# Turning the next tile's tokens: TensorE's transposes against VectorE's 32x32 transposes and a way through DRAM

## The chip, the cores and the metric

One core of a Trainium2 chip runs the whole program. The time is device microseconds of one execution, as the median of several runs; the profiler gives one execution in detail. The engines are TensorE (PE, with its weight loads PEld), VectorE (DVE), ScalarE (ACT), GpSimd (POOL) and SyncE (SP), which here issues every DMA.

## The reference

For 8 batches of 576 tokens with 8 heads of 64: attention of 32 pack tokens over the keys, and of the queries over the packed values; the heads are joined to 512 features. Then a mixing step (real part of a Fourier transform over tokens and features, added to x), a normalization of each token, and a feed-forward net with its input added again:

```
X = np.fft.fft(np.fft.fft(x, axis=1), axis=2)
u = x + np.real(X)
un = (u - mean(u)) / sqrt(var(u) + 1e-6)
out = u + np.maximum(un @ w_ch1, 0.0) @ w_ch2        # w_ch1 512 x 2048, w_ch2 2048 x 512
```

All of it is fp32.

## The kernel before

The 4608 tokens are handled as 36 blocks of 128, kept in `ubuf` (128 tokens x 512 features). Of each batch come four blocks, (E,0), (O,0), (E,1), (O,1), and of each pair of batches one more, R, with the tokens left over. Nine tiles, 0 to 8, take four blocks each, in that order, so a tile can straddle batches: tile 2 holds R of the first pair and three blocks of batch 2, tile 6 holds two blocks of batch 5, an R, and one of batch 6.

`ffn` is the feed-forward net of one tile, 16 turns (`j`) over the 2048 hidden features. Each fp32 factor is used as two fp32r parts, a high one and a low one (`split`: ScalarE casts the high part, then VectorE or GpSimd subtracts to get the low one), and each product takes three matmuls. In turn j, `up(j)` is 12 matmuls of 128x128 by 128x512 into the one PSUM buffer `ph`; ScalarE makes `hh` (relu, L653) and VectorE `hl` (L654) from it. Then `down(j-1)` is 12 matmuls into the accumulators `acc` (L664). `wsplits` splits the weights, two parts per turn, `wr_h` on ScalarE (L99) and `wr_l` on GpSimd (L100), with room for three weights at a time; each `next(splits)` is one of them.

`up` needs the tokens transposed, features on the partitions: `uh` and `ul`, 128 x 4 x 512, one buffer each. The class `Turned` makes them for the next tile at the end of this one: `less(i)` subtracts the mean (VectorE, L601, tile `un`), `moves(i)` are four TensorE transposes of 128x128 (L608, into PSUM `untp`), handed out one by one between the matmuls of `up(15)`, `down(14)` and `down(15)`, and `parts(i)` splits the result into `uh` (ScalarE) and `ul` (VectorE). The scale of the normalization is applied at the end of the tile (L700), where the output is stored too.

`front(b)` is everything ahead of that for batch b: attention, spectra, and the blocks `u`. It is a generator, run a piece at a time by `step(i)`, i from 0 to 31, two steps per turn, while the tile before is in `ffn`. For tiles from 1 on, front(t+1) begins at step 1; (E,0) and (O,0) come at step 26, (E,1) and (O,1) at step 28, and R in steps 0 and 2 of the next tile (`rest`). The order on TensorE, VectorE, ScalarE and GpSimd is that of the program text for all tiles but the first; each of the engines works off its list in order. `after(n, what)` puts work off by n steps: the squares of `statistics` come one step after the block, the power two steps after.

From step 12 to step 21 VectorE has the softmax's end and the folding of the weights (`m`, `a`, `f`, `r`, `h` in `ORDER`: L393 to L397, L425, L427, L437 to L468, L481 to L485). DMA loads of keys, values and queries (`kp`, `vt`, `qt`) are on SP's queue.

Of the kernel before, what the change touches and what calls it, by code (L numbers as in the profile page):

```python
# [9 lines left out]
F32 = mybir.dt.float32  # L10
# [3 lines left out]
ALU = mybir.AluOpType  # L14
AX = mybir.AxisListType

P = 128
# [4 lines left out]
DM = 512  # L22
# [24 lines left out]
STG0 = [-2, -2, -4, -4, -6, -6]  # L47
STG1 = [9, None, None]
LEAD = 2
NJ = 16  # L50
MANUAL = {getattr(mybir.EngineType, n) for n in ("PE", "DVE", "Activation", "Pool")}
NE = 289
# [25 lines left out]
def tile_kernel(ctx, tc, kpT, qT, v, w1, w2, tabC, tabS, tabR, tabB, tabT, sel, ident_d, out):  # L78
    nc = tc.nc
# [4 lines left out]
    work = ctx.enter_context(tc.tile_pool(name="work", bufs=2))  # L84
    small = ctx.enter_context(tc.tile_pool(name="small", bufs=2))
    ps = ctx.enter_context(tc.tile_pool(name="ps", bufs=3, space=bass.MemoryType.PSUM))
    psf = ctx.enter_context(tc.tile_pool(name="psf", bufs=1, space=bass.MemoryType.PSUM))

    spare = ["acc0", "acc1", "acc2", "acc3"]
    nbank = [0]  # L90
# [7 lines left out]
    def split(hi, lo, src, lo_eng=None):  # L98
        nc.scalar.copy(hi, src)  # L99
        (lo_eng or nc.vector).tensor_tensor(lo, src, hi.bitcast(F32), ALU.subtract)  # L100
# [7 lines left out]
    for h in range(4):  # L108
        nc.gpsimd.memset(bmask[h * NPK:(h + 1) * NPK, h:h + 1], 0.5)
    w1f = cpool.tile([P, NJ, DM], F32, name="w1f")  # L110
    w2f = cpool.tile([P, NJ, DM], F32, name="w2f")

    nc.scalar.activation(small.tile([P, 1], F32, tag="ri", name="warm"), mhalf, AF.Exp)
    ubuf = cpool.tile([P, NU, DM], F32, name="ubuf")
    stages = (STG0 + STG1 * 40)[:2 * NJ]

# [35 lines left out]
    def spot(n, part, shape):  # L152

        t = (w1f, w2f)[n].rearrange("p j n -> p (j n)")[:, (part % NJ) * DM:]
        size = shape[1] * shape[2]
# [13 lines left out]
    def load_weights(j):  # L169

        for n, dst in enumerate((w1f, w2f)):
            if (j, n) not in fetched:
                fetch(j, n)
            st = fetched.pop((j, n))
            low, high = st[:, :, 0], st[:, :, 1]
            c = dst[:, j, :].bitcast(I32)


            nc.scalar.activation(c.bitcast(F32), high.bitcast(F32), AF.Prelu, scale=REBIAS, alpha=-2.0 ** 32)  # L179
            nc.vector.tensor_scalar(c, c, 3, None, ALU.logical_shift_left)  # L180
            nc.vector.scalar_tensor_tensor(c, low, 29, c, ALU.logical_shift_right, ALU.bitwise_or)  # L181
# [2 lines left out]


    u_of, stat_of, place_of, free = {}, {}, {}, list(range(NU))

    def new_u(key):
        place_of[key] = free.pop(0)
        u_of[key] = ubuf[:, place_of[key], :]  # L190

        stat_of[key] = small.tile([P, 4], F32, tag="stat", name="stat", bufs=12)
# [3 lines left out]
    steps = [None]  # L196

    def after(n, what):

        if steps[0] is None:  # L200
            what()
        else:
            due.append((steps[0] + n, what))
# [7 lines left out]
    def statistics(key):  # L211
        st, u = stat_of[key], u_of[key]
        nc.vector.tensor_scalar(st[:, 1:2], st[:, 0:1], 1.0 / DM, None, ALU.mult)  # L213

        def squares():
            junk = work.tile([P, DM], F32, tag="tmp", name="junk", bufs=3)
            nc.scalar.activation(junk, u, AF.Square, bias=st[:, 1:2], scale=-1.0, accum_out=st[:, 2:3])  # L217

        def deviation():
            nc.vector.tensor_scalar(st[:, 2:3], st[:, 2:3], 1.0 / DM, 1e-6, ALU.mult, ALU.add)  # L220
            nc.gpsimd.tensor_tensor(st[:, 2:3], st[:, 2:3], mhalf, ALU.pow)

        after(1, squares)
        after(2, deviation)
# [365 lines left out]
    class Turned:  # L590
# [2 lines left out]


        def __init__(self, keys):
            self.keys, self.un, self.tp, self.hl = keys, {}, {}, None

        def less(self, i):
            key = self.keys[i]
# [12 lines left out]
        def parts(self, i):  # L612
            if self.hl is None:
                self.hl = [work.tile([P, 4, 512], F32R, tag=n, name=n, bufs=1) for n in ("uh", "ul")]
            w = slice(i * P, (i + 1) * P)
            split(self.hl[0][:, :, w], self.hl[1][:, :, w], self.tp[i].rearrange("p (c t) -> p c t", c=4))

    def wsplits():

        for _ in tiles:  # L620
            for n, j in [(0, 0)] + [x for j in range(1, NJ) for x in ((0, j), (1, j - 1))] + [(1, NJ - 1)]:
                hi = work.tile([P, DM], F32R, tag="wr", name="wr_h", bufs=6)
                lo = work.tile([P, DM], F32R, tag="wr", name="wr_l", bufs=6)
                split(hi, lo, (w1f, w2f)[n][:, j, :], nc.gpsimd)
                ready.append((hi, lo))
                yield

    def ffn(first, turned, step, nxt, alone):
        keys = turned.keys
        n = len(keys)  # L630
        T = n * P
        uh, ul = turned.hl
        acc = [psf.tile([P, DM], F32, tag=f"acc{i}", name=f"acc{i}") for i in range(n)]
        now["acc"] = acc

        def up(j, moves=(), between=lambda: None):
            moves = list(moves)
            wh, wl = ready.pop(0)

            pool, tag = (ps, "ps") if alone and j % 2 else (psf, "ph")  # L640
            ph = pool.tile([P, 512], F32, tag=tag, name="ph")

            step = T // 2 if first == 0 and j < SPL else T
            for t in (slice(i, i + step) for i in range(0, T, step)):
                for k in range(12):
                    c, (l, r) = k // 3, ((wh, uh), (wh, ul), (wl, uh))[k % 3]
                    nc.tensor.matmul(ph[:, t], l[:, c * P:(c + 1) * P], r[:, c, t], start=(k == 0), stop=(k == 11))  # L647
                    if moves:
                        moves.pop(0)()
            between()  # L650
            hh = work.tile([P, 512], F32R, tag="hh", name="hh")
            hl = work.tile([P, 512], F32R, tag="hl", name="hl")
            nc.scalar.activation(hh[:, :T], ph[:, :T], AF.Relu)  # L653
            nc.vector.scalar_tensor_tensor(hl[:, :T], ph[:, :T], 0.0, hh[:, :T].bitcast(F32), ALU.max, ALU.subtract)  # L654
            return hh, hl

        def down(j, hh, hl, moves=()):

            moves = list(moves)
            vh, vl = ready.pop(0)  # L660
            for i in range(n):
                w = slice(i * P, (i + 1) * P)
                for k, (l, r) in enumerate(((hh, vh), (hh, vl), (hl, vh))):
                    nc.tensor.matmul(acc[i], l[:, w], r, start=(j == 0 and k == 0), stop=(j == NJ - 1 and k == 2))  # L664
                    if moves:
                        moves.pop(0)()

        def less(*ks):
            for k in ks:
                nxt.less(k)  # L670

        prev = None
        for j in range(NJ):
            last = nxt is not None and j == NJ - 1
            if last:
                cur = up(j, nxt.moves(0) + nxt.moves(1), lambda: less(2, 3))
                nxt.parts(0)
                nxt.parts(1)  # L680
            else:
                cur = up(j)
            next(splits, None)
            if nxt is not None and j == NJ - 2:
                less(0, 1)
            step(2 * j)
            if prev is not None:
                down(j - 1, *prev, [lambda: None] * 8 + nxt.moves(2) if last else ())
                if last:
                    nxt.parts(2)  # L690
                next(splits, None)
            step(2 * j + 1)
            prev = cur
        down(NJ - 1, *prev, nxt.moves(3) if nxt else ())
        if nxt:
            nxt.parts(3)
        next(splits, None)
        for i, key in enumerate(keys):
            u = u_of[key]
            nc.vector.scalar_tensor_tensor(u, acc[i], stat_of[key][:, 2:3], u, ALU.mult, ALU.add)  # L700
            nc.sync.dma_start(out[(first + i) * P:(first + i + 1) * P, :], u)
            free.append(place_of[key])

    keys = []
# [10 lines left out]
    cur = Turned(tiles[0][1])  # L715
# [8 lines left out]
    rest = iter(())  # L724
    for j in range(ORDER[0].count("D"), LEAD):
        load_weights(j)
    ready, splits = [], wsplits()
    next(splits)
    next(splits)
    for t, (first, tk) in enumerate(tiles):  # L730
# [4 lines left out]
        def step(i):  # L735

            next_step()
            if t > 0 and i in (0, 2):
                next(rest, None)
            elif not ended and next(gen, None) == "rest":  # L740
                ended.append(gen)
            if t == 0 and i % 2 == 0 and i // 2 + LEAD < NJ:
                load_weights(i // 2 + LEAD)
            assert i < 2 * NJ - 1 or t + 1 >= B or ended

        nxt = Turned(tiles[t + 1][1]) if t + 1 < len(tiles) else None
# [3 lines left out]
        cur, rest = nxt, gen  # L750
# [101 lines left out]
```

## Time and profile before

| what | value |
|---|---|
| time, median of 3 runs | 1028.04 us (1027.53 to 1029.04) |
| profiled execution, first to last instruction | 1025.3 us |
| left between that span and the median of the runs | 2.7 us |
| TensorE busy | 978.5 us (95%) |
| VectorE, ScalarE, GpSimd busy | 608.8, 425.0, 463.1 us |
| L608, transposes of the tokens on TensorE | 144, 37.2 us of busy time |
| mean granted TensorE clock | 0.983 |

For the profiled execution the page gives the span alone, and the sums of the prediction are made against it. A row of the page or of a view that groups instructions names the line, the engine, the operation, what it writes and reads, the count, then the busy time and the mean of one in ns, then the idle time ahead of them and what ended it. A row of a timeline has the start in us, the duration in us, engine, line, operation, tiles, and in brackets how long the engine had been idle before and which instruction released it. Durations of matmuls overlap, since they are pipelined; the distance between starts is the time that one takes.

### The profile page before, as it was taken

The numbers are of one execution on the slowest core, as the hardware profiler recorded it, in microseconds if no ns is written. First come the engines' busy times: TensorE is split into PE (matmuls) and PEld (weight loads), VectorE is DVE, ScalarE is ACT, GpSimd is POOL, SyncE is SP. The second block draws the span as 40 slices with busy tenths as digits, with TensorE's granted clock in tenths as the row PEclk, the third lists the DMA queues.
The fourth block names the chain that finished last, engine by engine and source line by source line (L and its number), as shares of the span: only waits on it lengthen the run. The fifth ranks groups of instructions, "written<-read, shape, count | busy, mean of one in ns | idle before, by whom it ended". The sixth has DMA issues, their size and how long they took to land.

```text
span 1025.3 us, 14876 instructions
## 1 busy us (share of the span) xinstructions
PE 978.5 (95%) x5692; PEld 795.6 (78%) x5692; DVE 608.8 (59%) x1264; ACT 425.0 (41%) x883; POOL 463.1 (45%) x419
## 2 busy tenths in 40 slices
PE   6489889999999999999999999999999999999998
PEld 2367668878877888788887887788778888887886
DVE  3897994559465856677556846594658562114112
ACT  2556454444443434444444435444435343333322
POOL 1535635364335534454345533643355344444443
PEclk9699899999999999999999999999999999999999
DMA  8328440220023000310041002200210000001001
GB/s 329 109 64 280 157 123 1 93 96 1 1 78 111 1 1 34 108 48 1 1 140 49 1 1 93 96 0 1 82 58 0 1 26 17 0 1 43 1 1 42
DMA packets 17742, 58.64 MB, mean 57 GB/s; under 512 B 2081, under 2 KB 2465, under 8 KB 17670
## 3 DMA queue, kind: packets, MB, share of 16 engines
q1 hardware_dynamic: 17670, 57.68, 16.4%
q8 instruction: 45, 0.74, 0.3%
q14 instruction: 27, 0.22, 0.1%
HBM read 48.24 MB, written 9.44 MB: 56 GB/s over the span
## 4 chain that ended last, share of the span: by engine, by line
PE 76%; DVE 11%; ACT 5%; DMA 3%; issue 2%; POOL 2%; ACTq 0%; SPq 0%; DVEq 0%; POOLq 0%
PE ph L647 35%; PE acc L664 30%; DVE ubuf L567 2%; DMA wst<-w 2%; DVE turned L419 1%; ACT hh L653 1%; PE po L326 1%; PE s L269 1%; ACT junk L217 1%; DVE turned L415 1%; POOL wr_l L100 1%; PE e1tp L303 1%; DVE hl L654 1%; ACT wr_h L99 1%; DVE w2f L181 1%
## 5 line engine op out<-in xcount | busy, mean ns | idle before, releaser
L100 POOL TENSOR_TENSOR wr_l<-w1f,wr_h 128x512 fp32r<-128x512 f32 x144 | 190.8, 1325 | 398.9 <-ACT wr_h L99 395.1
L654 DVE SCALAR_TENSOR_TENSOR hl<-ph,hh 128x512 fp32r<-128x512 f32 x144 | 98.8, 686 | 305.3 <-ACT hh L653 305.0
L647 PE MATMUL ph<-uh,wr_h 128*128 128x512 f32 (+1 forms) x580 | 231.5, 399 | 11.8 <-DVE hl L654 9.6
L100 POOL TENSOR_TENSOR wr_l<-w2f,wr_h 128x512 fp32r<-128x512 f32 x144 | 192.4, 1336 | 91.9 <-ACT wr_h L99 91.9
L664 PE MATMUL acc<-wr_l,hh 128*128 128x512 f32 x576 | 227.0, 394 | 3.0 <-POOL wr_l L100 3.0
L647 PE MATMUL ph<-uh,wr_l 128*128 128x512 f32 (+1 forms) x580 | 229.3, 395 | 0.4 <-POOL wr_l L100 0.4
L647 PE MATMUL ph<-ul,wr_h 128*128 128x512 f32 (+1 forms) x580 | 229.3, 395 | 0.2 <-DVE ul L100 0.2
L664 PE MATMUL acc<-wr_h,hh 128*128 128x512 f32 x576 | 227.8, 396 | 0.0
L664 PE MATMUL acc<-wr_h,hl 128*128 128x512 f32 x576 | 226.2, 393 | 0.0
L653 ACT ACTIVATE hh<-ph 128x512 fp32r<-128x512 f32 x144 | 85.8, 596 | 285.6 <-PE ph L647 285.4
L647 PEld LDWEIGHTS ph<-uh,wr_h 128*128 128x128 f32 x580 | 109.9, 190 | 44.9 <-DVE hl L654 9.8
L647 PEld LDWEIGHTS ph<-uh,wr_l 128*128 128x128 f32 x580 | 110.0, 190 | 24.7 <-POOL wr_l L100 0.8
L664 PEld LDWEIGHTS acc<-wr_l,hh 128*128 128x128 f32 x576 | 108.2, 188 | 26.8 <-POOL wr_l L100 5.4
L647 PEld LDWEIGHTS ph<-ul,wr_h 128*128 128x128 f32 x580 | 110.0, 190 | 23.9 <-issue 1.7
L664 PEld LDWEIGHTS acc<-wr_h,hh 128*128 128x128 f32 x576 | 108.2, 188 | 23.5 <-ACT w2f L179 0.8
L664 PEld LDWEIGHTS acc<-wr_h,hl 128*128 128x128 f32 x576 | 108.2, 188 | 23.1
L99 ACT CAST wr_h<-w2f 128x512 fp32r<-128x512 f32 x144 | 89.4, 621 | 9.4 <-PE ph L647 7.8
L99 ACT CAST wr_h<-w1f 128x512 fp32r<-128x512 f32 x144 | 88.4, 614 | 8.0 <-PE ph L647 3.1
L217 ACT ACTIVATE junk<-ubuf,stat 128x512 f32<-128x512 f32 x36 | 25.8, 718 | 77.3 <-DVE stat L213 77.3
L608 PE MATMUL untp<-ident,un 128*128 128x128 f32 x144 | 37.2, 273 | 1.9 <-DVE stat L220 1.7
L100 POOL TENSOR_TENSOR gl<-turned,gh 128x516 fp32r<-128x516 f32 x16 | 25.2, 1573 | 22.1 <-ACT gh L99 22.1
L567 DVE SCALAR_TENSOR_TENSOR ubuf<-qe,pe 128x512 f32<-128x512 f32 x32 | 34.6, 1115 | 0.5
(199 smaller groups left out, 1292.8 us busy)
## 6 DMA issues: line engine op xcount, KB each, us to landing
kp<-kpT SPq DMA_DIRECT2D x16, 608.0 KB, 4.9
out<-ubuf SPq DMA_DIRECT2D x36, 256.0 KB, 2.1
vt<-v SPq DMA_DIRECT2D x14, 640.0 KB, 4.7
wst<-w SPq DMA_DIRECT2D x17, 512.0 KB, 4.0
qt<-qT SPq DMA_DIRECT2D x14, 576.0 KB, 4.8
ubuf<-w SPq DMA_DIRECT2D x9, 512.0 KB, 4.6
w1f<-w SPq DMA_DIRECT2D x3, 512.0 KB, 11.1
w2f<-w SPq DMA_DIRECT2D x3, 512.0 KB, 11.2
```

Source lines behind the costliest of these rows:

```text
L99: nc.scalar.copy(hi, src)
L100: (lo_eng or nc.vector).tensor_tensor(lo, src, hi.bitcast(F32), ALU.subtract)
L181: nc.vector.scalar_tensor_tensor(c, low, 29, c, ALU.logical_shift_right, ALU.bitwise_or)
L217: nc.scalar.activation(junk, u, AF.Square, bias=st[:, 1:2], scale=-1.0, accum_out=st[:, 2:3])
L269: nc.tensor.matmul(res[g][c][at, :w.stop - w.start], lhs(g, h), rhs(g, h, w), start=True, stop=True, tile_position=(r, h * NPK))
L303: nc.tensor.transpose(tp[g][:, c * P:(c + 1) * P], e1s[g][:, c * P:(c + 1) * P], ident)
L567: nc.vector.scalar_tensor_tensor(u_of[key], qe, sign, pe, ALU.mult, ALU.add, accum_out=stat_of[key][:, 0:1])
L608: nc.tensor.transpose(tp[:, c * P:(c + 1) * P], un[:, c * P:(c + 1) * P], ident)
L647: nc.tensor.matmul(ph[:, t], l[:, c * P:(c + 1) * P], r[:, c, t], start=(k == 0), stop=(k == 11))
L653: nc.scalar.activation(hh[:, :T], ph[:, :T], AF.Relu)
L654: nc.vector.scalar_tensor_tensor(hl[:, :T], ph[:, :T], 0.0, hh[:, :T].bitcast(F32), ALU.max, ALU.subtract)
L664: nc.tensor.matmul(acc[i], l[:, w], r, start=(j == 0 and k == 0), stop=(j == NJ - 1 and k == 2))
```

## The change

A block of the next tile whose statistics were begun in an earlier step is "sent" while the present tile is still in its turns: VectorE subtracts the mean and writes the result with its columns regrouped (each quarter of 32 within the four chunks of 128 together), transposes it in blocks of 32x32, one DMA writes it to DRAM, and four DMAs read it back, each to 32 partitions, so that the block arrives in SBUF with features on partitions. `send_next` is called after the odd steps 15 to 27 and once more after step 27, and sends the first block that is ready and hasn't gone; tile 0 doesn't call it.

By the order of the blocks this sends three of four blocks in tiles 1 and 2 (one at step 15, two at step 27), all four in tiles 3 and 4 (steps 15 and 17, two at 27), all in tiles 5 and 6 (steps 15, 17, 19, and one at 27), and all in tile 7 (steps 15, 17, 19, 21): 26 blocks. The other two of tiles 1 and 2, and those of tile 0 and of the first preparation, go through TensorE as before.

At the end of the tile a sent block has no `less` and no `moves`. Its `parts` read the returned block from SBUF. The first two `parts` follow up(15), then comes a weight's split; down(14) is followed by the next weight's split and then by the last two `parts`.

```diff
+SEND = (15, 27)
...
+    dr = ctx.enter_context(tc.tile_pool(name="dr", bufs=4, space=bass.MemoryType.DRAM))
...
+        meant[key] = steps[0] or 0          # in statistics(key)
...
+        def send(self, i):
+            key = self.keys[i]
+            un = work.tile([P, 4, 4, 32], F32, tag="tmp", name="unp", bufs=3)
+            nc.vector.tensor_scalar(un, u_of[key].rearrange("p (c q d) -> p q c d", c=4, q=4),
+                                    stat_of[key][:, 1:2], None, ALU.subtract)
+            t = work.tile([P, DM], F32, tag="ln", name="unt")
+            nc.vector.transpose(t, un.rearrange("p q c d -> p (q c d)"))
+            far = dr.tile([P, DM], F32, tag="far", name="far")
+            nc.sync.dma_start(far, t)
+            if i // 2 not in self.pairs:
+                self.pairs[i // 2] = work.tile([P, 2, 4, P], F32, tag="wst", name="back", bufs=2)
+            back = self.pairs[i // 2][:, i % 2]
+            for q in range(4):
+                nc.sync.dma_start(back[q * 32:(q + 1) * 32],
+                                  far[:, q * P:(q + 1) * P].rearrange("(b d) n -> d b n", b=4))
+            self.sent[i] = back
+
+        def send_next(self):
+            for i, key in enumerate(self.keys):
+                if i not in self.sent and meant.get(key, steps[0]) < steps[0]:
+                    self.send(i)
+                    break
...
             w = slice(i * P, (i + 1) * P)
-            split(self.hl[0][:, :, w], self.hl[1][:, :, w], self.tp[i].rearrange("p (c t) -> p c t", c=4))
+            if i in self.sent:
+                hi, lo = (x[:, :, w].rearrange("p c (b t) -> p c b t", b=4) for x in self.hl)
+                split(hi, lo, self.sent[i].rearrange("p b (c t) -> p c b t", c=4))
+            else:
+                split(self.hl[0][:, :, w], self.hl[1][:, :, w], self.tp[i].rearrange("p (c t) -> p c t", c=4))
...
             if last:
-                cur = up(j, nxt.moves(0) + nxt.moves(1), lambda: less(2, 3))
-                nxt.parts(0)
-                nxt.parts(1)
+                late = [i for i in range(4) if i not in nxt.sent]
+                assert len(late) in (0, 1, 4), late
+                early = late[:2] if len(late) == 4 else []
+                late = [i for i in late if i not in early]
+                cur = up(j, [m for i in early for m in nxt.moves(i)], lambda: less(*late))
+                ahead = [i for i in range(4) if i not in late]
+                for i in ahead[:2]:
+                    nxt.parts(i)
             else:
                 cur = up(j)
             next(splits, None)
-            if nxt is not None and j == NJ - 2:
+            if nxt is not None and j == NJ - 2 and not nxt.sent:
                 less(0, 1)
             step(2 * j)
             if prev is not None:
-                down(j - 1, *prev, [lambda: None] * 8 + nxt.moves(2) if last else ())
+                down(j - 1, *prev, [lambda: None] * 8 + nxt.moves(late[0]) if last and late else ())
+                next(splits, None)
                 if last:
-                    nxt.parts(2)
-                next(splits, None)
+                    for i in ahead[2:] + late[:1]:
+                        nxt.parts(i)
             step(2 * j + 1)
+            if nxt is not None and first and SEND[0] <= 2 * j + 1 <= SEND[1]:
+                nxt.send_next()
+                if 2 * j + 1 == SEND[1]:
+                    nxt.send_next()
             prev = cur
-        down(NJ - 1, *prev, nxt.moves(3) if nxt else ())
-        if nxt:
-            nxt.parts(3)
+        down(NJ - 1, *prev, nxt.moves(late[1]) if nxt and len(late) > 1 else ())
+        if nxt and len(late) > 1:
+            nxt.parts(late[1])
```

More of the change, by code (lines that the diff above doesn't have):

```diff
@@ L186, in tile_kernel @@
     u_of, stat_of, place_of, free = {}, {}, {}, list(range(NU))
+    meant = {}
     def new_u(key):
@@ L595, in __init__ @@
         def __init__(self, keys):
-            self.keys, self.un, self.tp, self.hl = keys, {}, {}, None
+            self.keys, self.un, self.tp, self.hl, self.sent, self.pairs = keys, {}, {}, None, {}, {}
+        def send(self, i):
[19 more added lines that the diff above has]
+                    break
         def less(self, i):
```

## The prediction

> **What bounds the kernel now.** I read the page first (busy shares, then the chain that ended last), then each engine's timeline at the end of one token tile (tile 5, which ends near 733 us), then VectorE's in the middle of that tile, then the transfers.
>
> ```profile
> span 1025.3 us, 14876 instructions
> ...
> PE 978.5 (95%) x5692; PEld 795.6 (78%) x5692; DVE 608.8 (59%) x1264; ACT 425.0 (41%) x883; POOL 463.1 (45%) x419
> ...
> PE 76%; DVE 11%; ACT 5%; DMA 3%; issue 2%; POOL 2%; ACTq 0%; SPq 0%; DVEq 0%; POOLq 0%
> ...
> L608 PE MATMUL untp<-ident,un 128*128 128x128 f32 x144 | 37.2, 273 | 1.9 <-DVE stat L220 1.7
> ```
>
> TensorE is busy 95% of the span and is 76% of the chain: what leaves it shortens the time, if nothing takes its place. L608 is the transposes in question, 16 for each of nine tiles. Their 273 ns are pipelined, so their worth is read from the pitch of the instructions around them. TensorE at that tile's end:
>
> ```profile
> 722.51 0.39 PE L647 MATMUL ph<-uh,wr_h 128*128 128x512 f32 x1
> ...
> 722.77 0.48 PE L647 MATMUL ph<-ul,wr_h 128*128 128x512 f32 x1
> ...
> 725.18 0.48 PE L647 MATMUL ph<-uh,wr_l 128*128 128x512 f32 x1
> ...
> 725.96 0.39 PE L647 MATMUL ph<-uh,wr_l 128*128 128x512 f32 x1
> 726.18 0.39 PE L664 MATMUL acc<-wr_h,hh 128*128 128x512 f32 x1
> ...
> 728.00 0.39 PE L664 MATMUL acc<-wr_h,hl 128*128 128x512 f32 x1
> ...
> 729.30 0.48 PE L664 MATMUL acc<-wr_h,hh 128*128 128x512 f32 x1
> ...
> 730.39 0.50 PE L664 MATMUL acc<-wr_l,hh 128*128 128x512 f32 x1 [0.50 <-POOL wr_l L100]
> ...
> 733.36 0.39 PE L647 MATMUL ph<-uh,wr_h 128*128 128x512 f32 x1
> ```
>
> From 726.18 to 728.00 lie eight plain pitches, 0.2275 each; from 722.77 to 725.18 seven with a transpose between, 0.344 each: a transpose costs 0.1165 us. The end of the tile (up(15), down(14), down(15), 36 matmuls) takes 733.36 - 722.51 = 10.85: 8.19 of matmuls, 16 x 0.1165 = 1.86 of transposes, and a hole of 730.39 - 729.30 - 0.344 = 0.75, where down(15)'s second matmul waits for GpSimd's low half of its weights.
>
> **The change part by part. What leaves TensorE.** 26 blocks are sent early (three of four in tiles 1 and 2, all in 3 to 7; none in tile 0), so 104 transposes go: 12.1 us by pitch. But the hole says that down(15) is timed by ScalarE and GpSimd, so I follow their chain.
>
> ```profile
> 726.92 0.57 ACT L653 ACTIVATE hh<-ph 128x512 fp32r<-128x512 f32 x1
> 727.39 1.05 ACT L99 CAST uh<-untp 128x512 fp32r<-128x512 f32 x2
> 728.34 0.63 ACT L99 CAST wr_h<-w2f 128x512 fp32r<-128x512 f32 x1
> ```
>
> ```profile
> 679.28 1.31 POOL L100 TENSOR_TENSOR wr_l<-w1f,wr_h 128x512 fp32r<-128x512 f32 x1 [2.88 <-ACT wr_h L99]
> 680.54 1.52 POOL L100 TENSOR_TENSOR wr_l<-w2f,wr_h 128x512 fp32r<-128x512 f32 x1
> ...
> 729.04 1.29 POOL L100 TENSOR_TENSOR wr_l<-w2f,wr_h 128x512 fp32r<-128x512 f32 x1 [4.88 <-ACT wr_h L99]
> 730.28 1.07 POOL L221 TENSOR_TENSOR stat<-stat,mhalf 128x1 f32<-128x1 f32 x2
> ```
>
> Before: up(15)'s last matmul starts at 725.96, hh at 726.92 (ScalarE was in the squares of the statistics until then); two casts; wr_h at 728.34; wr_l from 729.04 to 730.33; TensorE goes on 0.06 later. After: that last matmul starts at 722.51 + 11 x 0.2275 = 725.01, and hh 0.45 later, 725.46, an estimate that takes the squares as out of the way (VectorE, which feeds them, loses 1.93 us of subtractions ahead of them, below). With the pitches of these rows (0.47 to the casts, 0.95 for two, 0.70 to wr_l, 1.29 for it) wr_l ends at 728.87. TensorE would want it at 722.51 + 25 x 0.2275 = 728.20, so the hole stays, 0.73. Then 1.46 is won up to the hole (730.33 - 728.87) and three transposes behind it, 0.35: 1.81 a tile. In tiles 1 and 2 the four transposes left stand ahead of the hole and vanish in it. In tile 7, which prepares no further batch, I take it that no squares hold hh back: 8 x 0.1165 + 0.35 = 1.28. Together 6 x 1.81 + 1.28 = **12.1 less**. Without the hole it would be 7 x (1.86 + 0.75) = 18.3; if the new casts, from SBUF in runs of 32, were half as long again, 0.3 each, 7 x 0.6 = 4.2 of it would go.
>
> **The low halves at the tile's end.** VectorE's subtractions for ul read PSUM now and SBUF on both sides after. How such an operation stands beside GpSimd is to be seen in the middle of the tile:
>
> ```profile
> 678.88 0.65 DVE L654 SCALAR_TENSOR_TENSOR hl<-ph,hh 128x512 fp32r<-128x512 f32 x1
> 679.45 1.45 DVE L437 TENSOR_TENSOR eo<-a 128x287 f32<-128x287 f32 x1
> 680.82 1.56 DVE L438 TENSOR_TENSOR eo<-a 128x287 f32<-128x287 f32 x1
> ...
> 684.17 0.69 DVE L654 SCALAR_TENSOR_TENSOR hl<-ph,hh 128x512 fp32r<-128x512 f32 x1
> 684.77 1.53 DVE L481 SCALAR_TENSOR_TENSOR xl<-eo,xh 128x256 fp32r<-128x256 f32 x1
> ...
> 688.56 0.44 DVE L437 TENSOR_TENSOR eo<-a 128x287 f32<-128x287 f32 x1
> ...
> 690.10 0.67 DVE L654 SCALAR_TENSOR_TENSOR hl<-ph,hh 128x512 fp32r<-128x512 f32 x1
> 690.70 2.32 DVE L455 TENSOR_TENSOR f<-eo 128x45 f32<-128x45 f32 x4
> ...
> 719.15 0.69 DVE L654 SCALAR_TENSOR_TENSOR hl<-ph,hh 128x512 fp32r<-128x512 f32 x1 [3.38 <-ACT hh L653]
> 719.76 1.93 DVE L601 TENSOR_SCALAR un<-ubuf,stat 128x512 f32<-128x512 f32 x2
> ```
>
> The same L437 takes 0.44 alone and 1.45 from 679.45, where GpSimd's wr_l runs until 680.59; then the second wr_l takes 1.52 instead of 1.31. One waits for the other. The Trainium skill says so too (SBUF — State Buffer, Who interferes with whom): a VectorE instruction with two SBUF inputs and a GpSimd instruction that reads SBUF take turns, and with one SBUF input it mostly doesn't contend; the trace agrees, hl's 0.65 to 0.69 beside 1.45. After the change the second ul would run from 727.3 to 728.0 and the wr_l of the hole is due at 727.57: it may wait 0 to 0.6. I take 0.3 a tile, half: **2.1 more**. What is queued behind that wr_l on GpSimd, the powers of 730.28 and the next tile's first wr_l, isn't needed before up(0). The last two casts now stand behind that weight's wr_h (0.51 more): uh whole at 729.0, wanted at 731.4, covered by down(15).
>
> **VectorE in the middle of the tile.** Each send moves a subtraction there and adds a transpose:
>
> ```profile
> L601 DVE TENSOR_SCALAR un<-ubuf,stat x36: 468/478/1536, 56.5 to 926.6; 128x512 f32<-128x512 f32 x36
> ```
>
> ```profile
> L374 DVE STREAM_TRANSPOSE s<-s2T x16: 665/667/717, 22.9 to 762.1; 128x512 f32<-128x512 f32 x16
> ```
>
> That is 0.48 + 0.67 = 1.15, at worst 1.54 + 0.72 = 2.26; I take 1.1 (neighbours overlap a little). It stands just ahead of an hl, and the next up() can't start before that hl has read ph (one buffer). The starts:
>
> ```profile
> 680.62 0.39 PE L647 MATMUL ph<-uh,wr_h 128*128 128x512 f32 x1
> ...
> 686.06 0.39 PE L647 MATMUL ph<-uh,wr_h 128*128 128x512 f32 x1
> ...
> 691.50 0.39 PE L647 MATMUL ph<-uh,wr_h 128*128 128x512 f32 x1
> ```
>
> So the slack is 680.62 - 679.53 = 1.09 at step 15, 686.06 - 684.86 = 1.20 at 17, 691.50 - 690.77 = 0.73 at 19. VectorE has no idle time from 678.88 to 690.77, so a backlog could add up. But what comes behind each of these hl is mostly waiting for GpSimd (L437, L438, L481, L455: 1.45, 1.56, 1.53 and 2.32 long), and a late start ends at the same release: the send fills a wait. Step 15 (six tiles) costs 0.1 each for the handover, step 17 (four tiles) nothing, step 19 (tiles 5 and 6) 1.1 - 0.73 = 0.4 each: **1.4 more**. Without such cover each send costs its whole length, less 0.73 a tile.
>
> The sends at step 27 (ten) fall into the idle 3.38 ahead of the hl at 719.15: two take 2.2. Their cover gone, they would cost as at step 19. They replace the subtractions of 719.76 (1.93). Nothing is added for these, nor for tile 7's four, whose VectorE is busy 20.86 of 87.60 us:
>
> ```profile
> 846.00:933.60 87.60, 87.59 (x400) 71.98 (x399) 20.86 (x30) 28.72 (x55) 40.69 (x33) 1.00 0.01 5
> ```
>
> **Transfers.** 130 are added, all on SP's queue, a write and four reads for each send:
>
> ```profile
> kp<-kpT SPq DMA_DIRECT2D x16, 608.0 KB, 4.9
> out<-ubuf SPq DMA_DIRECT2D x36, 256.0 KB, 2.1
> ```
>
> ```profile
> SPq L701 <- DVE ubuf L700: 711.8, 34, 91.1
> ```
>
> SP waits up to 91 us at a time for the tile's output, so the sends block nothing there; the reads wait in SP's order for their write, and a second send waits behind them. The last pair: VectorE ready by 718.0, write 2.1, four reads between 2.1 and 4.9: 722 to 725, or 727 for the second of two, needed by the casts at 725.9 (first two blocks) and 727.9 (last two). Hidden, by a microsecond or more: 0.
>
> The sum is -12.1 + 2.1 + 1.4 = -8.6. The profiled span is 1025.3; the runs' median of 1028.04 is 2.7 longer, which I leave as it is: **1019.4 us**.
>
> **Rivals.** (1) *The low halves take turns with GpSimd again*: the third ul loses to the two powers (1.07) and the fourth to the next wr_l (1.30), running 0.6 each in between. From the late wr_l's end at 729.2 that is 1.07 + 0.6 + 1.30 + 0.6, ul whole at 732.8, where up(0)'s second matmul wants it at 729.23 + 12 x 0.2275 = 731.96: 0.84 x 7 = 5.9, time 1025.3. For it: the rows of L438 and L481; against: the powers are tiny. (2) *Slower: the sends aren't absorbed.* Tiles 1 to 6 send 12 blocks at steps 15 to 19; with X the length of one, the loss is 12 X - 6 x 0.73 (X = 1.1: 8.8, time 1026.8; X = 2.26: 22.7, time 1040.7), and it passes the gain (10.0 without the 1.4) at X = 1.2. For it: no idle time there, and the permuted read may be slower than 0.48. Against: the waits behind. (3) *Late transfers.* If the four reads were served one after the other at kp's 4.9 each, 19.6, a block sent at step 27 would be back at 716.9 + 2.1 + 19.6 = 738.6, 10.7 after it is needed, in six tiles: 64 more, 1083. Against: each moves 64 KB, kp 608. It takes reads of 11 us together to be late at all. A page of the Trainium skill speaks for slow reads (VectorE: DVE Perf Modes, The three transpose paths: a plain DMA that transposes by strides is 19 times slower than a transposing one, where the innermost destination stride is large); no row here shows it, and these runs of 512 bytes are contiguous on both sides. (4) *Better*: GpSimd isn't held up and the sends cost nothing: 1028.0 - 12.1 = 1015.9; the hole gone too, 1009.7.
>
> **Numbers.** Forecast 0.58 (1016.5 to 1022.5); rival 1 0.14; rival 2 0.16 (0.08 of it slower, 0.04 within 0.2%, 0.04 still faster); rival 3 0.03; rival 4 0.09. About 0.2% (2 us) is what a measurement can tell. Faster: 0.58 + 0.12 of rival 1 (the rest, 0.02, would have its waits twice as long) + 0.04 + 0.09 = 0.83. Same: 0.02 + 0.04 = 0.06. Slower: 0.08 + 0.03 = 0.11. The range 1014 to 1026 takes in forecast, rival 1 and most of 4.
>
> **What would show it.** L608 down from 144 to 40; the tile's end at 9.3 instead of 10.85, still with one wait for wr_l; hl at step 15 about 1 later after hh, up() barely waiting; at step 19 a wait of 0.4 for hl in two tiles; ul at 0.69 or, blocked, up to 2; reads landed before the casts. The forecast is wrong if TensorE's waits for hl add up to over 5 us, or if up(0) waits for ul.

## The result, and the profile after

| | before | changed |
|---|---|---|
| time, median | 1027.91 us (1027.53 to 1029.04, 4 runs) | 1020.45 us (1019.84 to 1021.36, 4 runs) |
| ratio to before | | 0.993 (95% interval 0.9915 to 0.9944) |
| profiled execution, span | 1025.3 us | 1017.7 us |

The change makes the kernel 7.5 us faster; 1019.4 was forecast. From the page of the changed kernel (lines of the program have moved by 2 to 41, so `hl` is L685, `up` L678, `down` L695, the splits L101 and L102), and below it its view of the transposes' tile:

```profile
span 1017.7 us, 14984 instructions
...
PE 967.4 (95%) x5588; PEld 785.3 (77%) x5588; DVE 611.7 (60%) x1290; ACT 425.3 (42%) x883; POOL 469.4 (46%) x419
...
PE 70%; DVE 14%; issue 7%; POOL 4%; ACT 3%; DMA 1%; ACTq 0%; POOLq 0%; SPq 0%; DVEq 0%
...
far<-unt SPq DMA_DIRECT2D x26, 256.0 KB, 2.0
back<-far SPq DMA_DIRECT2D x104, 64.0 KB, 2.0
```

```profile
L635 PE MATMUL untp<-ident,un x40: 270/272/329, 56.0 to 400.7; 128*128 128x128 f32 x40
```

The 104 transposes are gone (144 to 40). VectorE's share of the chain rose from 11% to 14%. A share of the chain isn't time lost: the rise lies in tiles 5 and 6 (27.4 us of the chain in each, 8.5 before), while in tiles 1 to 4 VectorE has less of it (3.4 instead of 8.5 to 9.7); what the sends cost is in the table below. The 7% of "issue" (2% before) isn't a new cost either: the rise lies in tile 7 (51 us), where the chain was followed back along another engine, while TensorE starts an up() every 5.44 us there as before. The write and each of the reads land in 2.0 us.

The end of tile 5 on TensorE, with the same stations as before (start of up(15), of down(14), down(15)'s first and second matmul, start of the next tile's up(0)):

```profile
718.34 0.39 PE L678 MATMUL ph<-uh,wr_h 128*128 128x512 f32 x1
...
721.06 0.39 PE L695 MATMUL acc<-wr_h,hh 128*128 128x512 f32 x1
...
723.78 0.39 PE L695 MATMUL acc<-wr_h,hh 128*128 128x512 f32 x1
724.99 0.50 PE L695 MATMUL acc<-wr_l,hh 128*128 128x512 f32 x1 [0.82 <-POOL wr_l L102]
...
727.61 0.39 PE L678 MATMUL ph<-uh,wr_h 128*128 128x512 f32 x1
```

It takes 727.61 - 718.34 = 9.27 instead of 10.85. No matmul is slowed between 718.34 and 723.78, and the one wait that was foreseen is there: the second matmul of down(15) is 724.99 - 723.78 - 0.23 = 0.98 late, for the low half of its weights. ScalarE and GpSimd ahead of it:

```profile
721.26 0.60 ACT L684 ACTIVATE hh<-ph 128x512 fp32r<-128x512 f32 x1 [1.23 <-PE ph L678]
721.75 1.13 ACT L101 CAST uh<-back 128x512 fp32r<-128x512 f32 x2
722.78 0.62 ACT L101 CAST wr_h<-w2f 128x512 fp32r<-128x512 f32 x1
```

```profile
723.48 1.45 POOL L102 TENSOR_TENSOR wr_l<-w2f,wr_h 128x512 fp32r<-128x512 f32 x1 [3.92 <-ACT wr_h L101]
```

hh, two casts, wr_h, wr_l, one behind the other, ScalarE free 1.23 before hh: the squares are out of its way. Before the change hh stood right behind them, with no idle time between:

```profile
726.21 0.71 ACT L217 ACTIVATE junk<-ubuf,stat 128x512 f32<-128x512 f32 x1
726.82 0.19 ACT L217 ACTIVATION_READ_ACCUMULATOR junk<-ubuf,stat 128x1 f32 x1
726.92 0.57 ACT L653 ACTIVATE hh<-ph 128x512 fp32r<-128x512 f32 x1
```

So hh begins 0.43 us after the start of up(15)'s last matmul instead of 0.96 to 0.97, in each of tiles 1 to 6; in tile 7, which has no squares there, it was 0.43 before too. Of the 1.6 us that a tile's end gets shorter, 0.53 are this wait of ScalarE.

The middle of the same tile on VectorE, with the three sends (unp, unt) ahead of three hl:

```profile
673.78 0.45 DVE L605 TENSOR_SCALAR unp<-ubuf,stat 128x512 f32<-128x512 f32 x1
674.26 0.71 DVE L608 STREAM_TRANSPOSE unt<-unp 128x512 f32<-128x512 f32 x1
674.90 0.65 DVE L685 SCALAR_TENSOR_TENSOR hl<-ph,hh 128x512 fp32r<-128x512 f32 x1
675.47 1.58 DVE L441 TENSOR_TENSOR eo<-a 128x287 f32<-128x287 f32 x1
676.98 0.45 DVE L442 TENSOR_TENSOR eo<-a 128x287 f32<-128x287 f32 x1
...
679.60 0.71 DVE L608 STREAM_TRANSPOSE unt<-unp 128x512 f32<-128x512 f32 x1
680.23 0.65 DVE L685 SCALAR_TENSOR_TENSOR hl<-ph,hh 128x512 fp32r<-128x512 f32 x1
...
685.76 0.71 DVE L608 STREAM_TRANSPOSE unt<-unp 128x512 f32<-128x512 f32 x1
686.40 0.65 DVE L685 SCALAR_TENSOR_TENSOR hl<-ph,hh 128x512 fp32r<-128x512 f32 x1
```

And TensorE's up() behind the first and the third of these:

```profile
675.29 0.39 PE L695 MATMUL acc<-wr_h,hl 128*128 128x512 f32 x1
675.70 0.47 PE L678 MATMUL ph<-uh,wr_h 128*128 128x512 f32 x1
676.01 0.39 PE L678 MATMUL ph<-ul,wr_h 128*128 128x512 f32 x1
...
687.20 0.47 PE L678 MATMUL ph<-uh,wr_h 128*128 128x512 f32 x1 [0.35 <-DVE hl L685]
```

hl of step 15 ends at 675.55 and up() starts 0.15 later, 675.70 - 675.29 - 0.23 = 0.18 late; its second matmul comes 0.31 behind the first instead of 0.23. Such a stall comes eight times in the changed kernel, six times behind step 15 and twice behind step 19, and each time up() starts 0.15 behind the end of hl and has a first pitch of 0.31. The stretches of the tiles, by the starts of up() in the traces:

| stretch, us | before | changed | less |
|---|---|---|---|
| tile's end (up(15) to the next up(0)), tiles 1 to 6 | 10.85 to 10.88 | 9.27 to 9.31 | 9.4 together |
| the same, tile 7 | 10.56 | 9.31 | 1.25 |
| up(8) to up(12), tiles 1 to 4 | 23.92 | 24.20 to 24.23 | -1.2 together |
| the same, tiles 5 and 6 | 23.92 | 24.85, 24.89 | -1.9 together |
| up(12) to up(15), up(0) to up(8), tiles 1 to 7 | | | within 0.1 in each tile |

Gain 10.7, loss 3.1: 7.6, as the spans say (1025.3 - 1017.7).

### The profile page after: what moved, and what is told of

Its sections match the earlier page's. It is cut to its first block, busy times and chain, and to the rows that moved or that the text cites. A ratio compares the mean times of both kernels' runs of the same rounds, so it can differ in the third digit from the quotient of the medians.

```text
span 1017.7 us, 14984 instructions
## 1 busy us (share of the span) xinstructions
PE 967.4 (95%) x5588; PEld 785.3 (77%) x5588; DVE 611.7 (60%) x1290; ACT 425.3 (42%) x883; POOL 469.4 (46%) x419
## 4 chain that ended last, share of the span: by engine, by line
PE 70%; DVE 14%; issue 7%; POOL 4%; ACT 3%; DMA 1%; ACTq 0%; POOLq 0%; SPq 0%; DVEq 0%
PE ph L678 32%; PE acc L695 26%; POOL wr_l L102 3%; DVE turned L423 1%; PE po L330 1%; PE s L273 1%; DVE hl L685 1%; DVE turned L419 1%; DMA wst<-w 1%; ACT hh L684 1%; PE px L241 1%; PE e1tp L307 1%; PE px L243 1%; PE px L242 1%; DVE ubuf L571 1%
## 5 line engine op out<-in xcount | busy, mean ns | idle before, releaser
L102 POOL TENSOR_TENSOR wr_l<-w1f,wr_h 128x512 fp32r<-128x512 f32 x144 | 191.3, 1330 | 396.5 <-ACT wr_h L101 394.4
L685 DVE SCALAR_TENSOR_TENSOR hl<-ph,hh 128x512 fp32r<-128x512 f32 x144 | 98.6, 685 | 306.5 <-ACT hh L684 306.5
L678 PE MATMUL ph<-uh,wr_h 128*128 128x512 f32 (+1 forms) x580 | 230.8, 398 | 12.9 <-DVE hl L685 10.8
L102 POOL TENSOR_TENSOR wr_l<-w2f,wr_h 128x512 fp32r<-128x512 f32 x144 | 193.3, 1342 | 83.9 <-ACT wr_h L101 83.9
L695 PE MATMUL acc<-wr_l,hh 128*128 128x512 f32 x576 | 225.9, 392 | 4.7 <-POOL wr_l L102 4.7
L678 PE MATMUL ph<-uh,wr_l 128*128 128x512 f32 (+1 forms) x580 | 227.7, 393 | 0.4 <-POOL wr_l L102 0.4
L678 PE MATMUL ph<-ul,wr_h 128*128 128x512 f32 (+1 forms) x580 | 227.6, 392 | 0.2 <-DVE ul L102 0.2
L695 PE MATMUL acc<-wr_h,hh 128*128 128x512 f32 x576 | 226.3, 393 | 0.0
L695 PE MATMUL acc<-wr_h,hl 128*128 128x512 f32 x576 | 225.2, 391 | 0.0
L678 PEld LDWEIGHTS ph<-uh,wr_h 128*128 128x128 f32 x580 | 109.9, 189 | 48.5 <-DVE hl L685 9.8
L695 PEld LDWEIGHTS acc<-wr_l,hh 128*128 128x128 f32 x576 | 108.2, 188 | 28.6 <-POOL wr_l L102 7.5
L678 PEld LDWEIGHTS ph<-uh,wr_l 128*128 128x128 f32 x580 | 110.0, 190 | 24.2 <-POOL wr_l L102 0.8
L678 PEld LDWEIGHTS ph<-ul,wr_h 128*128 128x128 f32 x580 | 110.0, 190 | 22.9 <-issue 1.7
L695 PEld LDWEIGHTS acc<-wr_h,hh 128*128 128x128 f32 x576 | 108.3, 188 | 22.8 <-ACT w2f L181 0.8
L695 PEld LDWEIGHTS acc<-wr_h,hl 128*128 128x128 f32 x576 | 108.2, 188 | 22.7
L101 ACT CAST wr_h<-w2f 128x512 fp32r<-128x512 f32 x144 | 89.3, 620 | 9.7 <-PE ph L678 8.1
L101 ACT CAST wr_h<-w1f 128x512 fp32r<-128x512 f32 x144 | 88.4, 614 | 8.1 <-PE ph L678 3.1
L102 POOL TENSOR_TENSOR gl<-turned,gh 128x516 fp32r<-128x516 f32 x16 | 25.2, 1572 | 22.1 <-ACT gh L101 22.1
L241 PE MATMUL py<-gh,fh 128*128 128x258 f32 x64 | 19.2, 307 | 16.4 <-ACT fh L483 15.3
L225 POOL TENSOR_TENSOR stat<-stat,mhalf 128x1 f32<-128x1 f32 x36 | 24.5, 692 | 13.2 <-DVE stat L224 13.1
```

The source lines that it names most:

```text
L241: nc.tensor.matmul(o, lh, rh, start=first, stop=False)
```

## The experiments

The theory after this result: the change gains at the tile's end, where ScalarE's order (hh, casts, wr_h) and GpSimd's wr_l time TensorE, and gives a part back in the middle of the tiles, where the sends stand ahead of hl on a VectorE with no idle time. The rivals: the transfers or VectorE's added work cost something elsewhere; the tile's end is timed by something else, such as ul. Each kernel starts from the changed one, unless it is said otherwise. Ratios are to the kernel before, run again beside each group of experiments (medians 1027.42 to 1028.13). The end of tile 0 (the start of the scaling of its output) lies between 186.9 and 189.1 us in the profiles, and why isn't known; each profile is one execution. So medians a microsecond or two apart are read with the stretches beside them.

**Sends where VectorE has idle time.**

```diff
-SEND = (15, 27)
+SEND = (23, 27)
```

> Blocks are sent after the odd steps 23 to 27 instead of 15 to 27, the rest is as in the changed kernel. Theory (the sends at steps 15, 17 and 19 cost 3.05 us of TensorE waiting for hl, because VectorE has no idle time there; it has at steps 23 to 27): 1020.4 - 3.0 = 1017.4, and no wait for hl is left in the middle of tiles 1 to 6. Rival (a send costs its length wherever it stands, or the transfers now arrive late): 1020.4 or slower.

Measured: 1016.61 us, ratio 0.9898 (0.9885 to 0.9911). up(8) to up(12) is 23.91 to 23.92 in all six tiles, as before the change, and the tile's end is unchanged (9.26 to 9.29). The loss of 3.1 was the sends at steps 15 to 19, and nothing else in the middle. (The span is 3.3 shorter than that of the changed kernel, of which 0.2 lies in tile 0; the median is 3.8 lower.)

**The sends alone, on the kernel before.** `send`, `send_next`, `meant` and their calls added to the kernel before; what comes back isn't read.

> The kernel before, with the sends of the change added at the same steps and their result not used: the tokens still go through TensorE's transposes. Theory (the sends cost only their waits in the middle of tiles 1 to 6, 3.05 us): 1027.9 + 3.1 = 1031.0, and the tile's end stays at 10.85. Rival (the sends' VectorE work and 130 transfers disturb other places too, so that the net gain hides a larger cost): 1033 or more, with new waits elsewhere; rival (they cost nothing): 1027.9.

Measured: 1030.95 us, ratio 1.0033 (1.0021 to 1.0045), 3.5 slower than before. up(8) to up(12) is 24.19 to 24.22 in tiles 1 to 4 and 24.87, 24.88 in 5 and 6, together 3.1; the tile's ends are 10.80 to 10.87, and 11.02 in tile 4. So the cost is the one seen in the changed kernel, in the same place.

**No sends at all.** This takes out what the sends do, mean and transposition included:

```diff
-            un = work.tile([P, 4, 4, 32], F32, tag="tmp", name="unp", bufs=3)
...
-            self.sent[i] = back
+            self.sent[i] = u_of[key].rearrange("p (b x) -> p b x", b=4)
```

> The sends do nothing: no subtraction, no VectorE transpose, no transfers; the splits at the tile's end read the untransposed blocks where they lie (so the mean and the transposition are left out). Theory (with the sends at steps 23 to 27 they cost nothing at all, so that only the tile's end counts): the same as the kernel with the sends late, 1016.6 within 0.5, tile's end 9.27. Rival (the sends still cost something through VectorE, SBUF or the queues): 1015.5 or less.

Measured: 1017.07 us, ratio 0.9897 (0.9882 to 0.9912); tile's end 9.27 to 9.30, up(8) to up(12) 23.92. Sends at steps 23 to 27 can't be told from no sends: 26 subtractions, 26 transposes and 130 transfers, all hidden.

**Twice the reads.**

```diff
-            for q in range(4):
+            for q in (0, 1, 2, 3) * 2:
```

> The changed kernel with every block read back twice, eight reads instead of four for each send. Theory (the transfers are hidden; in tiles 3 and 4 the second block of step 27 has about 2.5 us to spare): 1020.4 to 1021, at most a small wait of ScalarE's last casts in tiles 3 and 4. Rival (the reads' landing sets the tile's end): 3 us more in each of tiles 1 to 4, 1030 or more.

Measured: 1020.56 us, ratio 0.9923 (0.9906 to 0.9939); the tile's end stays at 9.25 to 9.28 in all seven tiles. One cast of ScalarE, at the end of tile 2, waits 0.67 for its reads, which TensorE doesn't feel. The transfers have cover, even at twice the reads.

**All the new casts ahead of the weights' split**, to move the supposed cause the other way:

```diff
-                for i in ahead[:2]:
+                for i in ahead if nxt.sent else ahead[:2]:
...
-                    for i in ahead[2:] + late[:1]:
+                    for i in ([] if nxt.sent else ahead[2:]) + late[:1]:
```

> The changed kernel with all returned blocks split right after up(15), ahead of the weights' split, instead of two. Theory (TensorE's wait in down(15) follows ScalarE's order): wr_h and wr_l come one pair of casts, 1.03, later in tiles 3 to 7 and one cast, 0.52, later in tiles 1 and 2: 1020.4 + 6.2 = 1026.6, most of the gain gone; tile's end 10.3. Rival (GpSimd's own queue sets it): 1020.4.

Measured: 1029.49 us, ratio 1.0016 (1.0007 to 1.0026). The tile's end is 10.45 to 10.49 in tiles 3 to 7 and 9.85, 9.87 in 1 and 2: 1.18 and 0.59 more than in the changed kernel, where 1.03 and 0.52 were expected. On TensorE, down(15) of tile 5 in this kernel:

```profile
729.15 0.49 PE L695 MATMUL acc<-wr_h,hh 128*128 128x512 f32 x1 [0.55 <-ACT wr_h L101]
730.82 0.50 PE L695 MATMUL acc<-wr_l,hh 128*128 128x512 f32 x1 [1.18 <-POOL wr_l L102]
```

Now down(15) waits for wr_h too. This order alone undoes the gain. The median is 2.9 above the expectation; of that the ends explain 0.8. The profiled span is 8.1 longer than that of the changed kernel: 7.0 at the ends, and 1.1 in a later end of tile 0 (188.4 instead of 187.3). The profiled execution is itself 1.4 below the median, so its stretches can't explain the rest, which stays open.

**The weights' split ahead of the casts.**

```diff
+                if nxt.sent:
+                    next(splits, None)
                 for i in ahead[:2]:
                     nxt.parts(i)
             else:
                 cur = up(j)
-            next(splits, None)
+            if not (last and nxt.sent):
+                next(splits, None)
```

> At the tile's end the split of down(15)'s weights is put ahead of the first two casts of the new tokens. Theory (the end of the tile is set by ScalarE's order: two casts, wr_h, then GpSimd's wr_l, for which TensorE waits 0.98 us in each of seven tiles): wr_l ends 1.0 earlier, the wait goes, 7 x 0.95 = 6.6 less than the changed kernel's 1020.4, about 1014. Rival (the last blocks' ul, 0.5 later and beside GpSimd, is next in line): up(0) of the next tile waits for ul instead, gain below 3, 1017.5 or more.

Measured: 1021.7 us, ratio 0.9948 (0.9936 to 0.996): no gain. The wait in down(15) did go, and the tile's end is 8.18 to 8.19 in tiles 3 to 7 (8.67 in 1 and 2); but up(0) to up(1) grew by 1.1 (by 0.55 to 0.57 behind tiles 1 and 2, and by 1.8 behind tile 7): 6.7 won and 7.3 lost. TensorE, GpSimd and VectorE in this kernel, at the end of tile 5:

```profile
727.55 0.39 PE L678 MATMUL ph<-uh,wr_h 128*128 128x512 f32 x1
727.77 0.39 PE L678 MATMUL ph<-ul,wr_h 128*128 128x512 f32 x1
728.96 0.50 PE L678 MATMUL ph<-uh,wr_l 128*128 128x512 f32 x1 [0.80 <-POOL wr_l L102]
```

```profile
723.46 1.30 POOL L102 TENSOR_TENSOR wr_l<-w2f,wr_h 128x512 fp32r<-128x512 f32 x1 [2.88 <-ACT wr_h L101]
726.06 1.59 POOL L225 TENSOR_TENSOR stat<-stat,mhalf 128x1 f32<-128x1 f32 x2 [1.29 <-DVE stat L224]
727.62 2.55 POOL L102 TENSOR_TENSOR wr_l<-w1f,wr_h 128x512 fp32r<-128x512 f32 x2
```

```profile
723.94 1.98 DVE L102 TENSOR_TENSOR ul<-back,uh 128x512 fp32r<-128x512 f32 x2 [0.34 <-ACT uh L101]
725.84 0.20 DVE L224 TENSOR_SCALAR stat<-stat 128x1 f32<-128x1 f32 x2
```

The wait moved to up(0)'s third matmul, and neither the theory nor its rival had the reason: GpSimd, done at 724.76, stood idle until 726.06 because its next instructions, the two powers of the statistics, wait for two tiny operations of VectorE, which stand behind two ul; only then comes the next tile's first wr_l.

**Both edits so far** (the split first, the sends late).

> Both edits, the weights' split first and the sends at steps 23 to 27. Theory (two separate places on TensorE's path): the gains add, 1020.4 - 6.6 - 3.0 = 1010.8. Rival (ul is next in line at the tile's end): 1014.5 or more.

Measured: 1017.87 us, ratio 0.9912 (0.9897 to 0.9928). The stretches of the two kernels stand side by side unchanged: 23.92 in the middle, 8.18 and then 6.69 to 6.73 instead of 5.61 to 5.63 (ends of tiles 3 to 5). The gain of the late sends is there, that of the order isn't. In its profile tile 0 ends 2.0 later than in that of the late sends alone, and the rest is 0.5 longer; the medians lie 1.3 apart.

**The power out of the way**, on top of both:

```diff
-        after(2, deviation)
+        after(3, deviation)
```

> The weights' split first, the sends at steps 23 to 27, and the power of the statistics three steps after the block instead of two. Theory (with the split first the wait of 0.98 only moved to up(0) of the next tile, because GpSimd's two powers, which wait for VectorE, stand ahead of that tile's first wr_l): with the powers behind it that wait goes too; the tile's end 8.2 (8.7 in tiles 1 and 2) and up(0) to up(1) back at 5.6: 1016.6 - 5 x 1.09 - 2 x 0.6 = 1010.0. Rival (VectorE's ul, or the turns that it takes with GpSimd, are next in line): 1014 or more.

Measured: 1014.07 us, ratio 0.9869 (0.9854 to 0.9883): a gain, but not all of it. up(0) to up(1) is 6.23 to 6.30 behind tiles 3 to 5 (5.61 would be undisturbed), and behind tile 7 it is 4.47 instead of 2.72, the largest loss. In this kernel, at the end of tile 5, VectorE, GpSimd and TensorE:

```profile
718.66 4.29 DVE L102 TENSOR_TENSOR ul<-back,uh 128x512 fp32r<-128x512 f32 x4 [0.34 <-ACT uh L101]
722.88 0.20 DVE L224 TENSOR_SCALAR stat<-stat 128x1 f32<-128x1 f32 x2
```

```profile
718.19 1.30 POOL L102 TENSOR_TENSOR wr_l<-w2f,wr_h 128x512 fp32r<-128x512 f32 x1 [1.77 <-ACT wr_h L101]
719.74 1.45 POOL L102 TENSOR_TENSOR wr_l<-w1f,wr_h 128x512 fp32r<-128x512 f32 x1 [0.26 <-ACT wr_h L101]
```

```profile
723.01 0.50 PE L678 MATMUL ph<-ul,wr_h 128*128 128x512 f32 x1 [0.33 <-DVE stat L224]
```

Four ul take 4.29 where two take 1.28 undisturbed: VectorE waits for each of GpSimd's two wr_l in between, and now up(0) waits for ul. That is the rival of this run. It is also how rival 1 of the prediction would end, up(0) waiting for ul, once the waits ahead of it are gone; but here the ul lose to two wr_l, and the powers, to which rival 1 had the third one lose, come after them.

**Those two low halves on VectorE**, on top of both edits, the power back at two steps:

```diff
-        for _ in tiles:
+        for k in range(len(tiles)):
...
-                split(hi, lo, (w1f, w2f)[n][:, j, :], nc.gpsimd)
+                at_end = (0 < k < len(tiles) - 1 and (n, j) == (1, NJ - 1)) or (k > 1 and (n, j) == (0, 0))
+                split(hi, lo, (w1f, w2f)[n][:, j, :], nc.vector if at_end else nc.gpsimd)
```

> The weights' split first and the sends at steps 23 to 27 (the power back at two steps), and the low halves of the two weights split at a tile's end (down(15)'s and the next tile's first) on VectorE instead of GpSimd. Theory (with the split first, what is left of the wait is the turns that VectorE's four ul, both inputs in SBUF, and GpSimd's two wr_l take: 4 x 0.61 + 2 x 1.30 = 5.0 us between 718.2 and 722.5): on VectorE alone they are 6 x 0.61 = 3.7, all waits at the tile's end go, end 8.2 (8.7 in tiles 1 and 2), up(0) to up(1) 5.6: 1016.6 - 5 x 1.09 - 2 x 0.6 = 1010.0. Rival (VectorE itself is too late, or GpSimd's powers still hold it): 1013 or more.

Measured: **1011.47 us**, ratio 0.9831 (0.9814 to 0.9848), the fastest of all. The tile's end is 8.16 in tiles 3 to 7, which is 36 matmuls and nothing else, 8.67 in 1 and 2 (four transposes left), up(0) to up(1) is back at 5.61 to 5.63 (2.72 behind tile 7). VectorE at the end of tile 5 in this kernel, six subtractions with no wait between them:

```profile
718.54 0.68 DVE L102 TENSOR_TENSOR wr_l<-w2f,wr_h 128x512 fp32r<-128x512 f32 x1
719.13 1.29 DVE L102 TENSOR_TENSOR ul<-back,uh 128x512 fp32r<-128x512 f32 x2
720.34 0.20 DVE L224 TENSOR_SCALAR stat<-stat 128x1 f32<-128x1 f32 x2
720.46 0.68 DVE L102 TENSOR_TENSOR wr_l<-w1f,wr_h 128x512 fp32r<-128x512 f32 x1
721.06 1.28 DVE L102 TENSOR_TENSOR ul<-back,uh 128x512 fp32r<-128x512 f32 x2
```

From the end of tile 0 to the last tile's output the profile is 6.8 us shorter than that of the late sends alone (814.6 against 821.4), where 6.65 was expected; the median is 1.5 above the expected 1010.0, with tile 0 ending 1.8 later.

## Why the prediction was right, point by point

- **The sum**: -8.6 forecast, -7.6 in the profiles, -7.5 in the medians. It is this near partly by luck: the tile's ends gained 0.7 more than forecast and the sends cost 1.7 more, and the two partly cancel. The mechanism held: the wait of down(15) for wr_l stays and times the tile's end, so the gain comes by way of ScalarE's and GpSimd's chain. That the sum over this chain is the 12.1 of 104 transposes by pitch is a coincidence: of the 1.81 a tile, 0.51 was hh coming out from behind the squares (measured 0.53), and no TensorE time.
- **The chain at the tile's end**: forecast with hh 2.95, wr_h 4.37 and the end of wr_l 6.66 (0.3 of waiting for VectorE included) after up(15)'s start; measured 2.92, 4.44 and 6.59. The casts from SBUF are a little slower (1.03 for two instead of 0.95), the wait is smaller (wr_l 1.45 instead of 1.29, so 0.16). The end was to be 9.34 and is 9.27. In tile 7 the forecast gain was 1.28 - 0.3 = 0.98, the measured one 1.25. Together the two terms -12.1 + 2.1 = -10.0 came out as -10.7.
- **The sends in the middle**: the term that was sized wrong, 1.4 against 3.1. The length of a send was right at these steps (1.1 forecast; 1.12 from unp to hl at step 15, 1.14 at steps 17 and 19), and so was the absorbing: at step 17 hl is no later than its own send makes it, since VectorE is through L441 and L442 only 0.16 later in the tile than through their counterparts before, though the send ahead of them took 1.12. What failed is the step "1.09 of slack against 1.1": the slack was counted from the end of hl to the start of up(), but up() needs 0.15 after hl has ended when it waits for it (675.55 to 675.70), and a stalled TensorE loses another 0.1 to get going. So step 15 cost 0.28 instead of 0.1 in six tiles, and step 19 0.65 instead of 0.4 in two.
- **Step 27, tile 7, transfers at zero**: right; the runs without sends, with late sends and with doubled reads show it. Between these sends and the output of the tile SP issued no other transfer in tiles 1 to 6. In tile 7 a send is longer than 1.1: each subtraction takes 1.53, as in the forecast's worst case, beside GpSimd's wr_l (rows below, step 15 of the changed kernel); the send then takes 2.3, which VectorE's idle time there covers.

```profile
877.74 1.31 POOL L102 TENSOR_TENSOR wr_l<-w1f,wr_h 128x512 fp32r<-128x512 f32 x1 [2.87 <-ACT wr_h L101]
877.80 1.53 DVE L605 TENSOR_SCALAR unp<-ubuf,stat 128x512 f32<-128x512 f32 x1
879.37 0.71 DVE L608 STREAM_TRANSPOSE unt<-unp 128x512 f32<-128x512 f32 x1
```

- **Rival 1** (up(0) waits for ul) didn't happen in the changed kernel, where the wait for wr_l comes first; the run with the power moved shows up(0) waiting for ul, once the waits for wr_l and the powers are out of the way. **Rival 2** (sends not absorbed) is not what happened: its loss for X = 1.1 was 8.8. **Rival 3** didn't happen: a read of 64 KB, in runs of 512 bytes, landed in 2.0. The rule of the Trainium skill beside it (VectorE: DVE Perf Modes, The three transpose paths) is about strides that these reads don't have. **Rival 4** (GpSimd isn't held up, the sends cost nothing) wasn't met on either side: GpSimd's wr_l took 0.16 longer a tile, and the sends cost 3.1.
- **Queued behind wr_l**: the prediction said that the powers and the next wr_l aren't needed before up(0). True as long as down(15) waits; in the run with the split first exactly that queue takes the wait over.

## What to carry to other kernels

Work taken off the engine that is busy 95% is worth, at most, what the pitch of its neighbours says and the waits that go with it; the gain ends at the next engine's queue; follow that queue in order of issue, with what each item waits for, before crediting it, and again after each wait that is removed (here wr_l, then the powers, then ul). Put added work where the engine that does it is idle, not where it is ready first: moving the same sends by up to four turns won back the 3.1 us that they cost. When you compare a delay with a slack, take the hand-over and the restart off the slack first.

## What was not expected of the hardware

- A TensorE that had to wait for hl began 0.15 us after hl's end, and its first pitch was 0.31 instead of 0.2275; a stall of 0.18 cost 0.28 to 0.31.
- A VectorE subtraction with both inputs in SBUF takes turns with GpSimd both ways, down to one-column operations: two powers took 1.06 undisturbed, 1.50 to 1.62 beside ul, and four ul took 4.29 beside two wr_l, where two take 1.28 undisturbed. Six subtractions on VectorE alone took 3.8 us, less than four there and two on GpSimd. A subtraction of the mean, with one input in SBUF, can wait too: 0.44 to 0.48 in tiles 1 to 6, 1.53 in tile 7 beside GpSimd's wr_l.
- The same 128x512 transpose on VectorE took 0.711 from SBUF, and 0.667 from PSUM before.
